# Linear attention feeding an MLP on one core: batch 0's k and v in nine-token rows, tails on alternate partitions, half of q moved to the weights' queue, and one weight block moved up in it

## The chip, the core and the metric

The kernel runs on one core of one Trainium2 chip. The metric is device time in microseconds (us) of that core for one call. A time is about 1.75 us longer than the span that the profile of the same execution shows (300.79 us and a span of 299.0 for the kernel before), so the two are never mixed here: "time" is the metric, "span" and every moment belong to a profile and count from the start of its span. Unless said otherwise, a moment is that of the one execution that was profiled.

## The reference, cut to what matters

```python
q, k, v: (8, 8, 576, 64) f32            # batch, heads, tokens, head size
phi(x) = concat(relu(x) * cos_w, relu(x) * sin_w)   # cos_w, sin_w depend on the token
q_p, k_p = phi(q), phi(k)
kv  = einsum('bhsf,bhsd->bhfd', k_p, v)
z   = sum over tokens of k_p
num = einsum('bhsf,bhfd->bhsd', q_p, kv)
den = einsum('bhsf,bhf->bhs', q_p, z) + 1e-6
x   = (num / den), heads side by side    # (4608, 512)
h   = x @ w_in                           # w_in (512, 2048)
out = relu(h)**2 @ w_out                 # w_out (2048, 512), out f32
```

576 tokens are four times 128 and 64 more. Those last 64 are the "tail" of each head.

## The kernel before

All products are in bf16. A fixed order of slots runs over eight batches: each slot is a piece of the first MLP product (`gemm1`, eight or ten slots for a batch) or of the second (`gemm2`), with pieces of the attention of later batches placed between them. Batch 0 has nothing to hide behind; its attention is the front of the kernel.

Loads come in three kinds. SyncE's queue brings k, v and q of batch 0. GpSimd's queue brings, in this order, the four blocks of w_in, then q, k, v of batch 1, then the four blocks of w_out, then batch 2. One small cast of v on GpSimd stands ahead of that queue as a gate, meant to hold its loads back behind those of batch 0: in the profile v landed at 11.24, the cast began at 11.29, and the queue's first load was issued at 11.73.

```python
    def load(src, nm, b, eng):
        main = inp.tile([P, H, J, D], F32, ...)      # token 4*p + j on partition p
        tail = inp.tile([P, HH, D], F32, ...)        # heads 0-3 on partitions 0-63, 4-7 on 64-127
        eng.dma_start(out=main, in_=src[b, :, 0:MAIN, :].rearrange("h (p j) d -> p h j d", j=J))
        for g in range(2):
            eng.dma_start(
                out=tail[g * TAIL : (g + 1) * TAIL, :, :],
                in_=src[b, g * HH : (g + 1) * HH, MAIN:S, :].rearrange("h p d -> p h d"),
            )
    ...
    with tc.manual_schedule():
        load_batch(0, nc.sync, "kvq")
        constants()
        warm(34)                                     # multiplies of zeros; the clock is 1.00 here
        for j in range(NS):
            att_k(0, j)
        att_v(0, J - 1, nc.gpsimd, H - 1, H)         # the gate
        ...
        for i in range(4):
            load_w1(i, 4)
        load_batch(1, nc.gpsimd, "qkv")
        for i in range(4):
            load_w2(i, 4)
        load_batch(2, nc.gpsimd, "qkv")
        att_kv(0, 0)
        att_kv(0, 1)
        ...                                          # q's features, num, x of the first half of batch 0
        for s in range(len(slots)):
            run(s)
```

The second product of batch 0 starts at slot 8. Slots 8 and 9 use w_out block 0 only; slot 10 is the first that uses block 1.

Of the kernel before, what the change touches and what calls it, by code (L numbers as in the profile page):

```python
# [15 lines left out]
FP = 512  # L16
# [3 lines left out]
def kernel(  # L20
# [37 lines left out]

    kqv = {}

    def load(src, nm, b, eng):
        main = inp.tile([P, H, J, D], F32, name=nm, tag=nm, bufs=2)
        tail = inp.tile([P, HH, D], F32, name=nm + "t", tag=nm + "t", bufs=2)
        eng.dma_start(  # L64
            out=main[:, :, :, :],
            in_=src[b, :, 0:MAIN, :].rearrange("h (p j) d -> p h j d", j=J),
        )
        for g in range(2):
            eng.dma_start(  # L69
                out=tail[g * TAIL : (g + 1) * TAIL, :, :],  # L70
                in_=src[b, g * HH : (g + 1) * HH, MAIN:S, :].rearrange("h p d -> p h d"),
            )
        kqv[nm, b] = (main, tail)

    def load_batch(b, eng, order):
        for nm in order:
            load({"k": k, "v": v, "q": q}[nm], nm, b, eng)

    def piece(nm, b, j):
        main, tail = kqv[nm, b]  # L80
        return main[:, :, j, :] if j < J else tail[:, :, :]
# [5 lines left out]
    cos_col = const.tile([P, J + 1], F32, name="cos_col")  # L87
    sin_col = const.tile([P, J + 1], F32, name="sin_col")

    def constants():  # L90
        sidx = const.tile([P, J + 1], F32, name="sidx")
        for p0, p1, c, n, base, mult in [
            (0, P, 0, J, 0, J),
            (0, TAIL, J, 1, MAIN, 1),
            (TAIL, P, J, 1, MAIN, 1),
        ]:
            nc.gpsimd.iota(
                sidx[p0:p1, c : c + n],
                pattern=[[1, n]],
                base=base,  # L100
                channel_multiplier=mult,
                allow_small_or_imprecise_dtypes=True,
            )
# [26 lines left out]
    vexts = []  # L130
    for i in range(2):
        vx = att.tile([P, J, H, E1], BF16, name=f"vext{i}")
        vxt = att.tile([P, HH, E1], BF16, name=f"vextt{i}")
        for t in (vx, vxt):
            ones = t[:, :, :, D:E1] if t is vx else t[:, :, D:E1]
            nc.vector.memset(ones, 1.0)
        vexts.append((vx, vxt))
    kps, kvzs, kzs, qps, tqs, qpTs, xs = {}, {}, {}, {}, {}, {}, {}
    nums, xts, xtails = {}, {}, {}
# [7 lines left out]
    def kp_of(b, j):  # L147
        if j == J:
            return cached(kps, (b, 1), [P, HH, F], "kpt", 1)
        return cached(kps, (b, 0), [P, J, H, F], "kp", 1)[:, j]  # L150
# [6 lines left out]
    def x_of(b, j):  # L157

        if j == J:
            return cached(xs, (b, 2), [P, 2, P], "xt", 2)  # L160
# [9 lines left out]
    def feat_cos(dst, src, j):  # L170
# [4 lines left out]
            scalar2=cos_col[:, j : j + 1],  # L175
# [4 lines left out]
    def feat_sin(dst, src, j):  # L180
        nc.scalar.activation(  # L181
            out=dst[:, :, D:F], in_=src, func=ACTF.Relu, scale=sin_col[:, j : j + 1]
        )
# [5 lines left out]
    def att_v(b, j, eng, h0=0, h1=H):  # L189
        copy = eng.copy if eng is nc.scalar else eng.tensor_copy  # L190
        vx, vxt = vexts[b % 2]
        if j == J:
            copy(out=vxt[:, :, 0:D], in_=piece("v", b, j))
        else:
            copy(out=vx[:, j, h0:h1, 0:D], in_=piece("v", b, j)[:, h0:h1, :])  # L195
# [9 lines left out]
    def fill(n):  # L205

        wm = ps_a.tile([P, 2, FP], F32, name="wm", tag="pa", bufs=1)
        for i in range(n):
            nc.tensor.matmul(
                out=wm[:, i % 2, :],  # L210
                lhsT=ident[:, :],
                rhs=zeros[:, :],
# [4 lines left out]
    def att_kv(b, part):  # L217
        vx, vxt = vexts[b % 2]
# [5 lines left out]



        for j in (0, 1) if part == 0 else range(2, NS):
            for hh in range(HH):
                for half in range(2):
                    h = half * HH + hh  # L230
                    if j < J:
                        lhsT, rhs = kp_of(b, j)[:, h, :], vx[:, j, h, :]
                    else:
                        p0, p1 = half * TAIL, (half + 1) * TAIL
                        lhsT, rhs = kp_of(b, j)[p0:p1, hh, :], vxt[p0:p1, hh, :]
                    nc.tensor.matmul(  # L236
                        out=kz[:, half, hh * E1 : (hh + 1) * E1],
                        lhsT=lhsT,
                        rhs=rhs,
                        start=(j == 0 and hh == 0),  # L240
                        stop=(j == J and hh == HH - 1),
                    )
        if part == 1:
            nc.scalar.copy(
                out=kvzs[b].rearrange("p (a h) e -> p a (h e)", a=2),
                in_=kz[:, :, 0 : HH * E1],
            )

    def att_feat(b, j, parts="cs"):
        for c in parts:  # L250
            f = feat_cos if c == "c" else feat_sin
            f(qp_of(b, j), piece("q", b, j), j)
# [15 lines left out]
    def att_qT_pe(b, j, apart=False):  # L268

# [3 lines left out]
        if apart:  # L273
            hi = ps_h.tile([P, HH, P], BF16, name="tqh", tag="hps", bufs=2)
            tqs[b, j].append(hi)
        elif nh == H:
# [14 lines left out]
    def att_num(b, j, early=False):  # L291
        qpT, kvz = qpTs[b, j], kvzs[b]
        if early:
            num = ps_h.tile([P, 2, FP], F32, name="num", tag="hps", bufs=2)
        else:
            num = ps_a.tile([P, 2, FP], F32, name="num", tag="pa", bufs=1)
# [321 lines left out]
```

## Time and profile before

| before | value |
|---|---|
| time, median of the first 3 executions | 300.75 us (300.23 to 300.79) |
| span of the profiled execution | 299.0 us |
| TensorE busy | 291.1 us, 97% of the span |
| VectorE, ScalarE, GpSimd busy | 46%, 51%, 16% |
| first `gemm1` multiply of batch 0 | 19.47 |
| first `gemm2` multiply, after a wait of 1.27 for w_out block 0 | 38.27 |
| slot 10, the first use of w_out block 1 | 41.74 |
| from there to the end of the span | 257.26 |

How to read it: TensorE is nearly always busy, so the time is the moment at which its unbroken train of multiplies starts plus the length of that train. The lines of the page that carry it stand in the prediction below.

### The profile page before, as it was taken

To read this page: it belongs to the slowest core of one execution; us is meant where nothing else is said; L and a number is where in the kernel's file an instruction comes from. 1 tells how busy PE (TensorE), PEld (TensorE's weight loads), DVE (VectorE), ACT (ScalarE), POOL (GpSimd) and SP (SyncE) were. 2 spreads that over 40 slices of the span, in tenths; PEclk is the share of its full clock that TensorE was granted. 3 is DMA by queue.
4 is the path that set the end of the run, shared out by engine and by line. 5 is a ranking of instruction groups with operands and counts; after the bars stand their busy time and mean duration, and the time that the engine had idled before them with its cause. 6 is when DMAs were issued, how large, how long until landed. Compare 5 with 4: busy or idle time off the path is not lost.

```text
span 299.0 us, 6477 instructions
## 1 busy us (share of the span) xinstructions
PE 291.1 (97%) x2701; PEld 202.3 (68%) x2701; DVE 136.6 (46%) x333; ACT 153.0 (51%) x213; POOL 47.8 (16%) x79
## 2 busy tenths in 40 slices
PE   8799989999999999999999999999999999999995
PEld 3379845889456984589654884589754894589544
DVE  2367654475648386228730287227740273024100
ACT  3465743666738554655554555555563552255311
POOL 1463404661121002000021001100021000100000
DMA  7999993999639987898568926898468115100021
GB/s 211 284 204 342 288 231 123 329 355 248 163 97 181 229 253 112 257 248 239 140 175 208 327 43 90 268 256 242 124 168 212 37 35 81 70 35 3 34 73 70
DMA packets 77069, 52.98 MB, mean 177 GB/s; under 512 B 52240, under 2 KB 71952, under 8 KB 77040
## 3 DMA queue, kind: packets, MB, share of 16 engines
q1 hardware_dynamic: 67120, 29.50, 42.2%
q0 software_dynamic: 9776, 22.94, 27.1%
q8 instruction: 21, 0.34, 0.5%
q10 hardware_dynamic: 144, 0.13, 0.1%
q14 instruction: 8, 0.07, 0.1%
HBM read 36.70 MB, written 9.44 MB: 154 GB/s over the span
## 4 chain that ended last, share of the span: by engine, by line
PE 86%; DMA 10%; POOL 1%; SPq 1%; issue 0%; ACT 0%; ACTq 0%
PE yps L413 40%; PE hps L378 38%; DMA q<-in_q_dram 5%; PE num L305 3%; DMA w2sb<-in_moe_w_out_dram 3%; DMA v<-in_v_dram 3%; PE kz L236 3%; PE yh L413 2%; POOL w1sb L117 1%; SPq L69 0%; PE tx L346 0%; PE tq L279 0%; POOL vt L69 0%; POOL vext L195 0%; SPq L64 0%
## 5 line engine op out<-in xcount | busy, mean ns | idle before, releaser
L378 PEld LDWEIGHTS <-w1sb 128*128 128x128 bf16 x1312 | 113.2, 98 | 12.1
L378 PE MATMUL hps<-xT,w1sb 128*128 128x256 bf16 (+1 forms) x1056 | 118.0, 269 | 0.0
L413 PE MATMUL yps<-w2sb,gT 128*128 128x512 bf16 (+1 forms) x496 | 110.4, 372 | 0.0
L386 ACT ACTIVATE rt<-hps 128x1024 bf16<-128x1024 f32 x72 | 73.7, 1024 | 59.2 <-DVE gT L393 32.8
L413 PEld LDWEIGHTS <-gT 128*128 128x128 bf16 x528 | 49.6, 98 | 54.0 <-DMA w2sb<-in_moe_w_out_dram 1.4
L393 DVE TENSOR_TENSOR gT<-rt 128x1024 bf16<-128x1024 bf16 x64 | 44.0, 688 | 82.8 <-ACT rt L386 82.8
L409 POOL DMA_DIRECT2D out_dram<-ysb x34 | 20.5, 605 | 176.2 <-ACT ysb L399 173.2
L399 ACT COPY ysb<-yps 128x512 f32<-128x512 f32 (+1 forms) x35 | 20.0, 575 | 55.3 <-PE yps L413 55.3
L181 ACT ACTIVATE qp<-q,sin_col 128x512 bf16<-128x512 f32 x32 | 21.9, 719 | 6.4 <-DMA q<-in_q_dram 6.4
L181 ACT ACTIVATE kp<-k,sin_col 128x512 bf16<-128x512 f32 x32 | 21.2, 714 | 3.1 <-DMA k<-in_k_dram 3.1
L319 DVE TENSOR_TENSOR x<-num,rden 128x512 bf16<-128x512 f32 x32 | 22.1, 691 | 1.1
L171 DVE TENSOR_SCALAR qp<-q,cos_col 128x512 bf16<-128x512 f32 x32 | 14.5, 492 | 11.7 <-DMA q<-in_q_dram 11.7
L315 DVE TENSOR_SCALAR den<-num 128x8 f32<-128x8 f32 (+1 forms) x40 | 6.6, 165 | 23.9 <-PE num L305 23.7
L171 DVE TENSOR_SCALAR kp<-k,cos_col 128x512 bf16<-128x512 f32 x32 | 15.1, 481 | 4.9 <-DMA k<-in_k_dram 4.9
L378 PE MATMUL hps<-xTt,w1sb 128*128 128x128 bf16 x256 | 15.3, 219 | 0.0
L413 PE MATMUL yps<-w2sb,gTt 128*128 128x512 bf16 x64 | 14.5, 379 | 0.0
L195 DVE CAST vext<-v 128x512 bf16<-128x512 f32 (+1 forms) x31 | 13.0, 425 | 2.9 <-DMA v<-in_v_dram 2.9
L305 PEld LDWEIGHTS <-qpT 128*128 128x128 bf16 (+1 forms) x240 | 10.3, 100 | 3.3 <-issue 1.7
L236 PEld LDWEIGHTS <-kp 128*128 128x128 bf16 x256 | 9.5, 97 | 4.4 <-issue 1.9
L201 PE MATMUL wm<-zeros 128*128 128x512 bf16 x42 | 10.9, 421 | 1.2 <-DVE zeros L86 1.2
L305 PE MATMUL num<-kvz,qpT 128*128 128x65 bf16 (+1 forms) x240 | 11.7, 194 | 0.0
L236 PE MATMUL kz<-vext,kp 128*128 128x65 bf16 x256 | 9.9, 193 | 1.6 <-DVE vext L195 1.6
(58 smaller groups left out, 132.6 us busy)
## 6 DMA issues: line engine op xcount, KB each, us to landing
out_dram<-ysb POOLq DMA_DIRECT2D x28, 256.0 KB, 3.9
k<-in_k_dram SPq DMA_DIRECT2D x5, 1024.0 KB, 6.2
v<-in_v_dram SPq DMA_DIRECT2D x5, 1024.0 KB, 6.7
q<-in_q_dram SPq DMA_DIRECT2D x5, 1024.0 KB, 5.9
q<-in_q_dram POOLq DMA_DIRECT2D x3, 1024.0 KB, 13.7
k<-in_k_dram POOLq DMA_DIRECT2D x3, 1024.0 KB, 10.1
v<-in_v_dram POOLq DMA_DIRECT2D x3, 1024.0 KB, 9.7
w1sb<-in_moe_w_in_dram POOLq DMA_DIRECT2D x4, 512.0 KB, 8.8
```

Of the source, the lines that this page charges most:

```text
L171: nc.vector.tensor_scalar(out=dst[:, :, 0:D], in0=src, scalar1=0.0, scalar2=cos_col[:, j : j + 1], op0=ALU.max, op1=ALU.mult,)
L181: nc.scalar.activation(out=dst[:, :, D:F], in_=src, func=ACTF.Relu, scale=sin_col[:, j : j + 1])
L195: copy(out=vx[:, j, h0:h1, 0:D], in_=piece("v", b, j)[:, h0:h1, :])
L236: nc.tensor.matmul(out=kz[:, half, hh * E1 : (hh + 1) * E1], lhsT=lhsT, rhs=rhs, start=(j == 0 and hh == 0), stop=(j == J and hh == HH - 1),)
L305: nc.tensor.matmul(out=out, lhsT=lhsT, rhs=kvz[:, half * HH + hh, :], start=True, stop=True)
L319: nc.vector.tensor_tensor(out=x_of(b, j).rearrange("p (b k) (l d) -> p b k l d", b=n, l=2), in0=n4[:, :, :, 0:D].rearrange("p b (k l) d -> ...
L378: nc.tensor.matmul(out=out, lhsT=w1sb[:, kb, hb * P : (hb + 1) * P], rhs=rhs, start=(kb == 0), stop=(kb == KB - 1),)
L386: nc.scalar.activation(out=rt[:, :, :], in_=hps[:, :, :], func=ACTF.Relu)
L393: nc.vector.tensor_tensor(out=dst, in0=rt[:, :, :], in1=rt[:, :, :], op=ALU.mult)
L399: nc.scalar.copy(out=ysb[:, c0:c1], in_=acc)
L409: eng.dma_start(out=dst, in_=ysb[p0 : p0 + n, c0:c1])
L413: nc.tensor.matmul(out=acc, lhsT=lhsT, rhs=w2sb[:, hb, c0:c1], start=(hb == 0), stop=(hb == HB - 1))
```

## The change

The intent is a faster front. k and v of batch 0 are loaded in rows of nine consecutive tokens (2304 bytes), 64 rows for each head, with heads 0 to 3 on even partitions and heads 4 to 7 on odd ones, so there are no separate tails and each load goes to every second partition. Because two heads then share one multiply, v is kept in two copies, each zero on the other head's partitions. q of batch 0 is split: the first half comes in four-token rows on SyncE's queue, the other half (0.52 MB) and q's tail (0.13 MB) move to GpSimd's queue. All tails of all batches go on alternate partitions too. Finally w_out block 0 moves ahead of k and v of batch 1. Cut to its core:

```diff
+    def load_tail(nm, b, eng):
         for g in range(2):
             eng.dma_start(
-                out=tail[g * TAIL : (g + 1) * TAIL, :, :],
+                out=tail_of(nm, b).rearrange("(p g) h d -> p g h d", g=2)[:, g],
                 in_=srcs[nm][b, g * HH : (g + 1) * HH, MAIN:S, :].rearrange("h p d -> p h d"),
             )
+    def load_rows(dst, src, n, h0, h1, eng):
+        for g in range(2):
+            eng.dma_start(
+                out=dst.rearrange("(p g) h j d -> p g h j d", g=2)[:, g, h0:h1],
+                in_=src[g * HH + h0 : g * HH + h1].rearrange("h (p j) d -> p h j d", j=n),
+            )
 ...
+    def of_half(eng, dst, src, g):                  # half_of is 1 on the partitions of half g, else 0
+        if eng is nc.scalar:
+            eng.activation(out=dst, in_=src, func=ACTF.Copy, scale=half_of[:, g : g + 1])
+        else:
+            eng.tensor_scalar_mul(out=dst, in0=src, scalar1=half_of[:, g : g + 1])
+    def v9(eng, h, g, j0=0, j1=J9):
+        of_half(eng, vext9(h)[:, g, j0:j1, 0:D], nine_of("v")[:, h, j0:j1, :], g)
 ...
-        load_batch(0, nc.sync, "kvq")
+        for nm, h0, h1 in (("k", 0, 2), ("k", 2, 4), ("v", 0, 2), ("v", 2, 3), ("v", 3, 4)):
+            load_nine(nm, h0, h1, nc.sync)
+        load_qa(nc.sync)
         constants()
+        ones_by_half()
-        warm(34)
+        warm(26)
 ...                                                 # features and masked copies by head pair
-        att_v(0, J - 1, nc.gpsimd, H - 1, H)
+        v9(nc.gpsimd, 2, 1, J9 - 1, J9)             # the gate, now on the third head pair of v
-        for i in range(4):
+        load_w1(0, 4)
+        load_qb(nc.gpsimd)
+        for i in range(1, 4):
             load_w1(i, 4)
-        load_batch(1, nc.gpsimd, "qkv")
-        for i in range(4):
+        load_batch(1, nc.gpsimd, "q")
+        load_w2(0, 4)
+        load_batch(1, nc.gpsimd, "kv")
+        load_tail("q", 0, nc.gpsimd)
+        for i in range(1, 4):
             load_w2(i, 4)
         load_batch(2, nc.gpsimd, "qkv")
 ...                                                 # kv of batch 0 in 36 multiplies of 130 columns,
                                                     # then q in four quarters of 64 tokens by 8 heads
```

## The prediction

> **What bounds the kernel now.** I read the windows view first, to see where TensorE is ever idle (columns: stretch, its length, then the busy time of each engine with its instruction count, clock, DMA share, GB/s).
>
> ```profile
> 0.00:1.20 1.20, 0.01 (x1) 0.01 (x1) 0.27 (x1) 0.00 (x0) 0.51 (x7) 1.00 0.00 0
> 1.20:11.75 10.55, 8.95 (x35) 3.67 (x36) 2.63 (x12) 5.13 (x9) 0.99 (x5) 1.00 0.95 294
> 11.75:19.47 7.72, 7.09 (x96) 4.40 (x95) 5.33 (x14) 4.95 (x9) 7.07 (x10) 1.00 1.09 197
> 19.47:37.00 17.53, 17.53 (x227) 16.03 (x224) 11.37 (x26) 10.95 (x14) 6.68 (x9) 1.00 1.13 299
> 37.00:38.27 1.27, 0.01 (x1) 0.00 (x0) 1.23 (x3) 1.27 (x3) 0.00 (x0) 1.00 1.25 208
> 38.27:60.00 21.73, 21.73 (x200) 13.62 (x201) 9.89 (x30) 9.96 (x17) 8.83 (x13) 1.00 0.84 229
> 60.00:126.50 66.50, 66.50 (x657) 45.77 (x655) 39.47 (x100) 40.59 (x60) 11.72 (x18) 1.00 0.87 210
> 126.50:278.40 151.90, 151.90 (x1401) 109.61 (x1400) 65.63 (x150) 76.04 (x97) 12.05 (x21) 1.00 0.59 149
> ```
>
> From 38.27 us to the last multiply TensorE has no gap at all, and the clock is full. So the kernel is a front of 38.27 us plus a fixed train of matmuls. A change to batch 0 is worth exactly the time by which that train starts earlier, and no more. Before 38.27 the multiplies that count are eight slots of the first MLP product of batch 0, from 19.47; warm-up and filler multiplies make up much of what precedes.
>
> Then the chain of waits (start, length, what), its early part:
>
> ```profile
> 2.70 8.54 DMA v<-in_v_dram
> 11.24 0.06 issue
> 11.29 0.50 POOL vext L195
> 11.79 3.08 POOL w1sb L117 x4
> 14.87 13.74 DMA q<-in_q_dram
> 28.61 0.28 issue
> 28.89 0.61 POOL vt L69
> 29.50 8.73 DMA w2sb<-in_moe_w_out_dram
> 38.23 0.05 issue
> 38.27 0.60 PE yh L413 x2
> ```
>
> The reader should see that attention of batch 0 is not on this chain. The chain is: v lands at 11.24; that releases one GpSimd cast, which gates the GpSimd DMA queue; this queue then moves w_in, batch 1 and w_out. TensorE's own order says the same (the bracket is idle time and its cause):
>
> ```profile
> 36.40 0.61 PE L279 MATMUL tq<-ident,qp 128*128 128x128 bf16 x8
> 38.27 0.60 PE L413 MATMUL yh<-w2sb,gT 128*128 128x512 bf16 x2 [1.27 <-DMA w2sb<-in_moe_w_out_dram]
> ```
>
> Making batch 0's attention faster alone would only lengthen this 1.27 us wait. What decides is when the weight blocks land.
>
> **Landing times before.** From issue times and times to landing (where two issues share one window, the answer gives their median, and I solve for the second): w_in blocks at 17.8, 20.5, 23.1, 25.6; q of batch 1 at 28.6 (tails 29.2); k at 32.4 (tails 32.85); v at 35.5 (tails 35.9); w_out blocks at 38.2, 40.8, 43.3, 45.9. So one weight block takes 2.5 to 2.6 us, a 1 MB batch tensor 2.65 to 3.2, a pair of tails 0.4 to 0.6. They land back to back: the queue is bandwidth-bound from about 14 us, when its first data flow, to 45.9.
>
> [...] 5.64 MB read between 25.6 and 40.8 is 371 GB/s, near the 351 GB/s of the SyncE loads at 7 to 12 us. [...] 351 GB/s at 3 to 5 us without tails, 278 at 5 to 7 us with 560 packets under 512 B. [...] The trace's x<-num multiply (N = 512) took 691 ns[...].
>
> **The change, part by part.**
>
> 1. SyncE loads. k and v come as nine-token rows of 2304 B: no separate tails, 2.36 MB; only half of q (0.52 MB) stays in this queue. Before, 3.54 MB ran from about 1.9 to 13.4 us, with 0.39 MB of tails costing 0.7 us more than large packets (0.39/0.22 - 0.39/0.37, an estimate from the rates above). Without that, 3.54 MB would take 10.8 us, 328 GB/s. With about 0.9 us from last byte to landing, estimates: first half of k 5.1, second 6.8, first half of v 8.4, the third head pair of v (which gates GpSimd) 9.1, last 10.1, half of q 11.7. Before: k 6.4, v 11.26, q 14.36.
>
> 2. Feature work. VectorE now does six two-input passes over 576 elements[...], and four masked copies at about 0.45 (a 512-element cast took 0.42): 6.3 us, begun at 5.1 with short waits, done near 11.7. ScalarE's nine small activations and four masked copies fit beside it. kv is 36 multiplies of 130 columns instead of 40 of 65, some 2 us, mostly hidden. Then the q part in four quarters: before, q landing to first MLP multiply took 19.47 - 14.36 = 5.1 us; quarters pipeline it but have more links, so I keep 5.1 from 11.8. First MLP multiply at 16.9, a gain of 2.6 us.
>
> 3. GpSimd queue. v gates it at 9.1, cast about 0.45, so w_in block 0 is issued at 9.55 instead of 11.73 and lands 6.1 later, 15.65. Behind it now comes the other half of q (0.52 MB in 512 B runs, about 1.75 us, estimated from half of a batch tensor and some loss). So the other w_in blocks land at 20.0, 22.55, 25.05: only 0.5 us earlier than before. Slots 1 to 3 of the first product want them at about 19.9, 22, 24.8. Hence slot 3 starts at about 25.1 (26.35 before): the gain shrinks from 2.6 to about 1.3 here.
>
> 4. w_out block 0 moves ahead of k and v of batch 1: it lands at 25.05 + 3.0 + 0.6 + 2.4 = 31. Slot 3 to the end of the first product took 36.99 - 26.35 = 10.64, so w_out is wanted at 35.7; the 1.27 us wait goes. But block 1 still stands behind k, v, their tails and now also q's tails of batch 0: 31 + 3.2 + 0.45 + 2.7 + 0.4 + 0.5 + 2.5 = 40.8. It is wanted two slots of 1.73 us after 35.7, at 39.2. Before, that slot began at 38.27 + 3.46 = 41.73 with its block there at 40.8. So the wait moves from block 0 to block 1: 1.6 us of new wait, and the train is 41.73 - 40.8 = 0.9 us ahead of before.
>
> 5. After that, block 2 lands near 43.3 and is wanted after 45; no wait. Tails of the other seven batches: 4 multiplies of 130 columns for 8 of 65, even; two ScalarE copies of kv for one, a masked VectorE copy more: beside TensorE. Batch 2's q load now waits until q's tail of batch 0 is used (about 48 us, was issued at 34.1), lands near 54 and is wanted near 59. No cost, but the margin shrinks.
>
> [...]
>
> **Rivals.**
> (a) The front gain passes through whole: 2.6 + 1.27 = 3.9 us, 296.9 us. For it: w_out block 0 really is early. Against: w_in and w_out block 1 land hardly earlier, as the back-to-back landings say.
> (b) w_out block 1 does not bind, only w_in: slot 10 at 39.2, gain 2.5, 298.2 us. It needs the queue 1.6 us faster than I add it up[...].
> (c) v lands no earlier than before[...], so block 1 lands at 42 or later: gain 0 or a loss of up to 1 us.
> (d) VectorE's 6.3 us, or a semaphore chain among the quarters, delays the first multiply beyond 19.5. It would take an error over 2.6 us; unlikely, and up to 1 us of it is free because w_in binds.
> (e) The program orders each GpSimd transfer behind the landing of the one eight before it (before, kt waited 2.0 us for w_in this way). w_out block 1 now waits so for k of batch 1; if nothing else is queued meanwhile, the queue runs dry for up to 1 us. v and the tails should cover it.
>
> **Range and chances.** 300.75 - 1.1 gives 299.6. Full success of (b) gives the low end, 298.2; (c) and (e) in part give the high end, 300.8. Two per cent is 6 us, more than the whole front gain of (a), and a loss of 6 us would need a new stall in the steady part: faster 0.01, same 0.98, slower 0.01.
>
> **What would show it right or wrong.** Right: v's third part releases GpSimd near 9.1 to 9.6; the first MLP multiply near 17; a TensorE wait on w_in of some tenths before slots 1 to 3; no wait before the first yh multiply, near 35.7; a wait of 1 to 2 us on w_out before the second block, near 40.8; and no gap afterwards. Wrong: a first MLP multiply later than 18.5; no w_out wait at all (then (b) or (a)); a wait on k or v of batch 1 or on q of batch 2; TensorE gaps after 60 us; or strided tail weights that lengthen the tail groups of eight multiplies beyond their 0.25 us.

The marks in it stand for passages that are cut because no trace or run of this case shows what they say. Step 2's 6.3 us was six passes at 0.757 us and four copies at 0.45; the changed kernel's six passes took 0.748 to 0.759 each in its trace. Step 4's sum comes to a gain of 0.9 us (299.85); terms that are cut rounded it up to 1.1 us, and so to the 299.6 of the range. The rate behind 0.39/0.22 in step 1 stands nowhere above it; the nearest measured one is 211 GB/s, from 5.8 to 6.0 us, where 110 of the 126 packets were under 512 B. The "about 0.9 us from last byte to landing" fits q, whose queue moved data until about 13.4 and which landed at 14.36. The "some 2 us" for kv fits the 1.73 us that eight multiplies of 512 columns take in this trace: at that rate 36 of 130 columns would take 1.98.

## The result, and the profile after

The changed kernel is correct. Its time is 301.58 us, median of 4 executions (300.69 to 301.85), against 300.50 (300.23 to 300.79) for the kernel before in the same rounds. The ratio is 1.0031, with a 95% interval of 1.0006 to 1.0055. A ratio here is always the mean time of one kernel's fast executions over that of the other's of the same rounds, so it is not quite the ratio of the medians quoted. The class is "same", as predicted; the size is not: a gain of 1.1 us was predicted, and a small loss came, outside the range.

The profiled execution was the changed kernel's fastest one (300.69; span 298.9). The windows view of the changed kernel, in the stretches shown of the kernel before (columns: stretch, length, busy time and instruction count of TensorE, its weight loads, VectorE, ScalarE and GpSimd, then clock, DMA share, GB/s), with two finer stretches at the end:

```profile
1.20:11.75 10.55, 8.10 (x36) 3.60 (x37) 6.86 (x22) 7.11 (x16) 2.37 (x8) 0.98 0.84 273
11.75:19.47 7.72, 7.18 (x95) 5.89 (x94) 4.97 (x13) 3.21 (x8) 6.68 (x9) 0.80 1.04 200
19.47:37.00 17.53, 17.06 (x219) 15.59 (x218) 12.40 (x32) 11.66 (x16) 6.27 (x10) 1.00 1.13 290
37.00:38.27 1.27, 1.27 (x16) 1.09 (x15) 0.83 (x3) 0.71 (x2) 0.60 (x1) 1.00 1.06 233
...
8.60:11.06 2.46, 0.01 (x2) 0.00 (x1) 2.46 (x5) 1.98 (x3) 1.02 (x2) 1.00 0.93 306
11.06:15.70 4.64, 4.64 (x46) 4.37 (x46) 2.63 (x5) 2.72 (x7) 4.64 (x7) 0.63 0.88 157
```

Two things are new. The hole at 37.00 to 38.27 is filled, as predicted. And the clock, which was 1.00 throughout before, is 0.80 in the second stretch. The finer rows show where: from 8.60 to 11.06 TensorE did nothing, while VectorE was busy all the time; in the 4.6 us after it, TensorE ran at a mean clock of 0.63 (it was 0.50 from 11.37 to 14.79). That the idle time brought this about is tested by warm38 below. TensorE's timeline of the changed kernel (start, length, group, and in the bracket the idle time before it and what ended it):

```profile
11.06 1.87 PE L338 MATMUL kz<-vext,kp 128*128 128x130 bf16 x18 [2.45 <-DVE vext L232]
...
20.20 0.61 PE L600 MATMUL hps<-xT,w1sb 128*128 128x128 bf16 x8 [0.46 <-ACT xT L465]
...
37.99 0.38 PE L639 MATMUL yh<-w2sb,gT 128*128 128x512 bf16 x1
...
41.85 0.59 PE L639 MATMUL yh<-w2sb,gT 128*128 128x512 bf16 x2
```

and slot 10 on TensorE's timeline of the kernel before:

```profile
41.74 0.59 PE L413 MATMUL yh<-w2sb,gT 128*128 128x512 bf16 x2
```

The first `gemm1` multiply comes at 20.20, 0.7 us later than before and 3.3 us later than predicted. The second product starts at 37.99 with no wait. Slot 10 starts at 41.85 without a wait, 0.11 us later than before. So the train has gained nothing.

The early chain of waits of the changed kernel, taken from a query that ends at 21 us (start, length, what), shows what leads to that late first multiply:

```profile
2.87 4.50 DMA k<-in_k_dram
...
7.47 1.58 DVE kp L304 x3
9.04 0.44 issue
9.48 1.54 DVE vext L232 x2
11.02 0.04 issue
11.06 1.87 PE kz L338 x18
...
14.74 0.62 PE kzh L338 x9
...
18.45 0.59 ACT qpTp L430
```

The second half of k lands at 7.37 (VectorE had waited 1.17 us for it), VectorE works through features and masked copies until 11.02, kv runs at the low clock until 15.36, and only then do the steps of q follow. q's first half had landed by 12.4 (two transfers, at 11.7 and 12.4): it is not on this chain. VectorE's timeline shows the size of the masked copies in the changed kernel:

```profile
9.48 1.52 DVE L232 TENSOR_SCALAR vext<-v,half_of 128x576 bf16<-128x576 f32 x2
```

and of the plain casts in the kernel before:

```profile
11.26 1.14 DVE L195 CAST vext<-v 128x512 bf16<-128x512 f32 x3 [2.92 <-DMA v<-in_v_dram]
```

Two copies of 576 elements take 1.52, so 0.76 each; three casts (two of 512 elements and one of 448, which the group's line hides) take 1.14, so 0.38 each, as they overlap a little (one lasts 0.41 to 0.47 by itself). GpSimd's timeline in the changed kernel gives the queue:

```profile
9.95 0.45 POOL L232 TENSOR_SCALAR vext<-v,half_of 128x64 bf16<-128x64 f32 x1 [8.02 <-DMA v<-in_v_dram]
...
35.35 2.24 POOL L198 DMA_DIRECT2D w2sb<-in_moe_w_out_dram  x3 [2.44 <-DMA k<-in_k_dram]
48.91 0.90 POOL L99 DMA_DIRECT2D q<-in_q_dram  x1 [11.31 <-DVE qp L277]
```

The gate opens at 9.95 rather than 9.1. w_in block 0, issued at 10.48, lands at 16.2; the moved half of q at 17.9; the last w_in block at about 26.1; q of batch 1 at 29.2; w_out block 0 at 32.0; k of batch 1 at 35.1. w_out block 1, issued at 35.35, takes 6.5 to land: about 41.8. That is the very moment at which slot 10 starts. Two ends therefore meet there: TensorE reaches slot 10 at about 41.8, and the block lands at about 41.8.

### The profile page after: what moved, and what is told of

Its sections match the earlier page's. It is cut to its first block, busy times and chain, and to the rows that moved or that the text cites. A ratio compares the mean times of both kernels' runs of the same rounds, so it can differ in the third digit from the quotient of the medians.

```text
span 298.9 us, 6467 instructions
## 1 busy us (share of the span) xinstructions
PE 289.2 (97%) x2655; PEld 204.2 (68%) x2677; DVE 144.6 (48%) x357; ACT 154.6 (52%) x229; POOL 50.3 (17%) x87
## 3 DMA queue, kind: packets, MB, share of 16 engines
q0 software_dynamic: 10016, 23.60, 29.2%
## 4 chain that ended last, share of the span: by engine, by line
PE 93%; DVE 2%; DMA 2%; ACT 1%; issue 1%; SPq 1%; ACTq 0%; DVEq 0%
PE hps L600 42%; PE yps L639 39%; PE num L514 3%; PE kz L385 2%; PE yh L639 2%; DMA k<-in_k_dram 2%; PE tq L491 1%; SPq L108 1%; PE kz L338 1%; PE kz L396 1%; PE kzh L338 1%; DVE kp L304 1%; PE tx L566 1%; DVE vext L232 1%; PE kz L365 0%
## 5 line engine op out<-in xcount | busy, mean ns | idle before, releaser
L639 PE MATMUL yps<-w2sb,gT 128*128 128x512 bf16 (+1 forms) x476 | 107.7, 372 | 1.2 <-DVE qpTp L500 0.2
L287 ACT ACTIVATE qp<-q,sin_col 128x512 bf16<-128x512 f32 (+1 forms) x34 | 22.3, 693 | 7.5 <-DMA q<-in_q_dram 7.5
L287 ACT ACTIVATE kp<-k,sin_col 128x512 bf16<-128x512 f32 (+1 forms) x35 | 21.5, 670 | 0.0
L277 DVE TENSOR_SCALAR qp<-q,cos_col 128x512 bf16<-128x512 f32 (+1 forms) x34 | 15.3, 485 | 11.5 <-DMA q<-in_q_dram 11.5
L277 DVE TENSOR_SCALAR kp<-k,cos_col 128x512 bf16<-128x512 f32 (+1 forms) x35 | 15.9, 453 | 0.0
L300 DVE CAST vext<-v 128x512 bf16<-128x512 f32 x28 | 11.8, 421 | 0.0
L514 PE MATMUL num<-kvz,qpT 128*128 128x65 bf16 (+1 forms) x240 | 11.7, 194 | 0.0
L639 PEld LDWEIGHTS <-gTt 128*128 128x128 bf16 x64 | 6.3, 98 | 7.5
L385 PEld LDWEIGHTS <-kp 128*128 128x128 bf16 x224 | 8.5, 97 | 2.4
L639 PE MATMUL yh<-w2sb,gT 128*128 128x512 bf16 x30 | 9.1, 379 | 0.1
```

The source lines that it names most:

```text
L277: nc.vector.tensor_scalar(out=dst[:, :, 0:D], in0=src, scalar1=0.0, scalar2=cos_col[:, c : c + 1], op0=ALU.max, op1=ALU.mult,)
L287: nc.scalar.activation(out=dst[:, :, D:F], in_=src, func=ACTF.Relu, scale=sin_col[:, c : c + 1])
L300: nc.vector.tensor_copy(out=vext_of(b, j)[:, :, 0:D], in_=piece("v", b, j))
L385: nc.tensor.matmul(out=kz[:, a, c0 : c0 + E1], lhsT=kp_of(b, j)[:, h, :], rhs=vext_of(b, j)[:, h, :], start=(j == 0 and c == 0 and g == 0) ...
L514: nc.tensor.matmul(out=out, lhsT=lhsT, rhs=kvz[:, half * HH + hh, :], start=True, stop=True)
L639: nc.tensor.matmul(out=acc, lhsT=lhsT, rhs=w2sb[:, hb, c0:c1], start=(hb == 0), stop=(hb == HB - 1))
```

## The experiments

The theory after reading the result: the mechanism of the prediction is right (the time is the start of slot 10 plus a fixed train), but two chains both end too late, the front because of the masked copies and the lost clock, and w_out block 1 because the queue ahead of it is longer than added up. Then repairing one of them should gain nothing. Rivals: the loss is VectorE's masked copies alone; the lost clock alone; the late gate alone; the reorder of w_out; or something in the steady part. Twelve runs were made in four calls; the kernel before was run beside them in each call (medians 300.61, 300.49, 301.08, 300.57). All twelve were correct.

This table collects the moment that the argument turns on. Span minus slot 10 is the length of the rest of the train; each row is one profiled execution.

| kernel | first `gemm1` multiply | wait for w_out block 1 | slot 10 starts | span | span minus slot 10 |
|---|---|---|---|---|---|
| before | 19.47 | none (1.27 for block 0) | 41.74 | 299.0 | 257.3 |
| changed | 20.20 | none | 41.85 | 298.9 | 257.1 |
| after_again | 20.75 | none | 42.38 | 299.4 | 257.0 |
| split8 | 20.28 | 0.85 | 42.92 | 300.0 | 257.1 |
| warm38 | 19.10 | 1.60 | 42.65 | 300.6 | 258.0 |
| w2b | 19.13 | none | 40.76 | 298.6 | 257.8 |
| before_w2up | 18.70 | none | 39.90 | 297.2 | 257.3 |
| gate_v0 | 18.92 | 1.10 | 42.80 | 300.4 | 257.6 |
| combo | 18.29 | 1.63 | 42.12 | 299.1 | 257.0 |
| qb_twice | 20.67 | 1.25 | 44.51 | 301.6 | 257.1 |
| q_sync | 20.14 | 0.99 | 42.92 | 299.6 | 256.7 |
| q_sync_warm | 19.14 | none | 40.80 | 297.5 | 256.7 |
| no_reorder | 21.98 | 1.83 for block 0 | 45.27 | 302.3 | 257.0 |
| w2up_spare | 18.40 | 0.37 | 41.59 | 298.9 | 257.3 |

Slot 10 ranges over 5.4 us, from 39.90 to 45.27, while the rest stays between 256.7 and 258.0. In the profiled executions, that rules out a cost of the change in the steady part: the two profiles of the changed kernel have 257.1 and 257.0, less than the 257.3 before. (warm38, w2b and gate_v0 have 0.5 to 0.9 us more in the rest, each in its one profiled execution.)

### after_again: the changed kernel, unchanged

No edit; it shows how much the changed kernel scatters.

> The changed kernel, unchanged, to see how it varies: its first profile was its fastest execution (300.69 us; the other three 301.45 to 301.85). There the second w_out block landed at 41.85 us, just when TensorE came to it. Theory B (two ends meet: the train of matmuls waits either for the first MLP product or for w_out block 1, whichever is later): a slower execution shows a TensorE wait of 0.5 to 1 us on w2sb near 42 us. Theory A (only the slow start of the first product counts): a slower execution shows the first hps multiply later than 20.2 us, and no w2sb wait. Median 301 to 301.8, ratio 1.001 to 1.004.

Measured: 301.21 us (301.01 to 302.15, 6 executions), ratio 1.0027 (1.0005 to 1.0048). The profiled execution has its first multiply at 20.75 and slot 10 at 42.38, with no wait for w_out, whose block 1 landed at about 42.2. Here the front is what ends last, by 0.2 us; in the first profile the two met. The small loss is real (the interval leaves out 1), and its two ends lie within half a microsecond of each other.

### split8: VectorE's masked copies cut into eight rows and one

```diff
     def v9(eng, h, g, j0=0, j1=J9):
-        of_half(eng, vext9(h)[:, g, j0:j1, 0:D], nine_of("v")[:, h, j0:j1, :], g)
+        cuts = [(j0, j1)] if eng is not nc.vector else [(0, J9 - 1), (J9 - 1, J9)]
+        for a, z in cuts:
+            of_half(eng, vext9(h)[:, g, a:z, 0:D], nine_of("v")[:, h, a:z, :], g)
```

> VectorE's four masked nine-row copies are cut into 8 rows and 1 row. They took 0.76 us each where 8-row casts take 0.42. Expected: 8-row part about 0.42 to 0.45, 1-row part 0.12 to 0.2, so kv starts at 10.3 to 10.7 instead of 11.06, and the first hps multiply comes 0.4 to 1.5 us before 20.2 (the larger figure if TensorE keeps its full clock). Theory A: the time falls by the same. Theory B: w_out block 1 still lands near 41.9, so the time stays within 0.3 us of the changed kernel, and a w2sb wait of the size of the head start appears near 42 us.

Measured: 302.09 us (301.69 to 302.61), ratio 1.0052 (1.0029 to 1.0076). From VectorE's timeline of this kernel:

```profile
10.35 1.20 DVE L232 TENSOR_SCALAR vext<-v,half_of 128x512 bf16<-128x512 f32 x4
```

and from TensorE's:

```profile
42.92 0.59 PE L641 MATMUL yh<-w2sb,gT 128*128 128x512 bf16 x2 [0.85 <-DMA w2sb<-in_moe_w_out_dram]
```

Four shorter copies take 1.20 where two long ones took 1.52, and the stretch from VectorE's first pass over the second half of k to the first kv multiply is 3.11 instead of 3.59. So the nine-row copies do cost what the trace says, yet the time did not fall: slot 10 was ready at 42.07 by TensorE's order and waited 0.85 for the block. The rival "masked copies alone" falls, since the block came last here. The expectation of an earlier front missed, though: in this execution k's second half landed at 8.2 instead of 7.4, so kv began at 11.44 and the first multiply came at 20.28, no earlier than in the changed kernel. What the copies are worth in the front was therefore not seen at the first multiply. The time is also some 0.9 us above the changed kernel's, where at most 0.3 was expected. In this kernel the gate's cast took 0.85 instead of 0.45 on GpSimd, so the queue was released later.

### warm38: 38 warm-up multiplies instead of 26

```diff
-        warm(26)
+        warm(38)
```

> 38 warm-up multiplies instead of 26, so TensorE is not idle from 8.6 to 11.06 us. Expected: granted clock 1.0 in 11 to 15 us (it was 0.5 from 12 to 14), kv and its fillers take about 3 us instead of 4.5, and the first hps multiply comes at 18.5 to 19.2 instead of 20.2. If the clock drop was only a side effect of VectorE being late anyway, less than 0.4 us moves. Theory A: the time falls by 1 to 1.7 us. Theory B: it falls by less than 0.3 us, with a w2sb wait near 42 us.

Measured: 301.69 us (301.44 to 302.33, 5 executions), ratio 1.0038 (1.0016 to 1.0061). From the windows of this kernel, its kv stretch:

```profile
11.59:14.60 3.01, 3.01 (x44) 2.86 (x44) 2.49 (x5) 2.33 (x6) 3.01 (x5) 1.00 0.77 93
```

and TensorE's timeline:

```profile
19.10 0.61 PE L600 MATMUL hps<-xT,w1sb 128*128 128x128 bf16 x8 [0.46 <-ACT xT L465]
...
42.65 0.59 PE L639 MATMUL yh<-w2sb,gT 128*128 128x512 bf16 x2 [1.60 <-DMA w2sb<-in_moe_w_out_dram]
```

The clock is 1.00, kv with its fillers takes 3.0 us instead of 4.6, and the first multiply comes 1.1 to 1.65 us earlier than in the two profiles of the changed kernel. The gain went into the 1.60 us wait for w_out block 1. The rival "lost clock alone" falls as well; so says the changed kernel's one execution that kept a mean clock of 1.0, too: it took 301.45, in the middle of the 300.69 to 302.15 of its nine others. (This execution of warm38, its slowest, also lost some 0.9 us after slot 10; where was not found.)

### w2b: w_out block 1 moved ahead of v of batch 1

```diff
-        load_batch(1, nc.gpsimd, "kv")
+        load_batch(1, nc.gpsimd, "k")
+        load_w2(1, 4)
+        load_batch(1, nc.gpsimd, "v")
         load_tail("q", 0, nc.gpsimd)
-        for i in range(1, 4):
+        for i in range(2, 4):
             load_w2(i, 4)
```

and, so that v is not wanted too early, kv of batch 1 goes from slot 10 to 11, its first two `num` steps from 11 and 13 to 12 and 13, and the first transpose of x from 12 to 13.

> w_out block 1 moved ahead of v of batch 1 in the GpSimd queue; kv of batch 1 one slot later, and its first num and transpose one slot later, to allow for v's later landing. The front is untouched, so the first hps multiply stays at 20.2. w_out block 1 lands about 3 us earlier, near 38.5, and v near 42. Theory B: the slow executions vanish, median about 300.7 (0.8 below the changed kernel), no w2sb wait. Theory A: unchanged, 301.4 to 301.7. If v is now late, a wait on vext appears before kz near 45 us.

Measured: 300.89 us (300.37 to 301.97), ratio 1.0015 (0.9989 to 1.0040). Block 1 landed at 38.2 and nothing waits for it. The six executions fall in two groups: 300.37, 300.42 and 300.42 at clocks of 0.997 to 1.000, and 301.35, 301.87 and 301.97 at 0.994. So the slow executions did not vanish, as had been expected. A drop to 0.50 for 3.4 us takes about 0.6% off the mean over 300 us, which is the 0.994. With the block out of the way the time is set by the front, and the front depends on the clock. Its profiled execution is a fast one: there TensorE's warm-ups lasted longer (until 9.89 instead of 8.61), it idled 1.69 us before kv instead of 2.45, and the clock held. The other profiles agree. After an idle time before kv of 1.69 us or less (warm38 0.55, gate_v0 1.19, the kernel before 1.60) the clock stayed at 1.00 there; after 2.18 (q_sync), 2.25 (split8), 2.45 and 3.03 (the changed kernel), 2.47 (qb_twice) and 3.83 (no_reorder) it fell to 0.50 for 3.4 us or more. So in these kernels the lost clock goes with how long the idle time before kv happens to be. The rest of the train was some 0.7 us longer here, with a wait of 0.67 in a `num` step of batch 1 that the moved slots brought.

### before_w2up: the kernel before, with only w_out block 0 moved up

```diff
-        load_batch(1, nc.gpsimd, "qkv")
-        for i in range(4):
+        load_batch(1, nc.gpsimd, "q")
+        load_w2(0, 4)
+        load_batch(1, nc.gpsimd, "kv")
+        for i in range(1, 4):
             load_w2(i, 4)
```

> The kernel before with the reorder alone: w_out block 0 ahead of k and v of batch 1. Block 0 then lands near 31 and the 1.27 us wait of TensorE on w2sb before the first yh goes, so the first yh comes at 37.0. Block 1 still lands near 40.8 (the same bytes in front of it as before); it is wanted at 37.0 + 3.46 = 40.46. Theory B (landing of w_out block 1 sets the train): a w2sb wait of about 0.4 us before the second block, time 0.9 us below before, 299.7. Theory A (the wait of 1.27 was the only cost): 299.3, no w2sb wait. A rival: the wait moves whole, time as before.

Measured: **299.35 us** (298.99 to 299.92), ratio 0.9944 (0.9903 to 0.9986). This beats both kernels: 1.14 us under the 300.49. TensorE's timeline of this kernel:

```profile
18.70 1.95 PE L378 MATMUL hps<-xT,w1sb 128*128 128x128 bf16 x32
...
39.90 0.59 PE L413 MATMUL yh<-w2sb,gT 128*128 128x512 bf16 x2
...
41.63 1.14 PE L236 MATMUL kz<-vext,kp 128*128 128x65 bf16 x32
```

kv of batch 1, which follows slot 10 and needs v of batch 1, starts at 41.63 with no bracket, so nothing waited: not for w_out block 1 (issued at 29.51, landed at 39.6, wanted at 39.90) and not for the delayed v. The one wait of TensorE between 17 and 50 us is 0.2 us on a VectorE copy. The reorder did what step 4 of the prediction says for block 0, and here block 1 is just in time. In this profile, its fastest execution, the first multiply also came 0.77 us earlier than in the profile of the kernel before, which the edit does not touch; so the 1.14 us of the medians, and not the 1.84 us between the two slots 10, is the measure of what the reorder is worth.

### gate_v0: GpSimd's gate on the first half of v

```diff
-        for g in range(2):
-            v9(act, 1, g)
+        v9(act, 1, 0)
+        v9(act, 1, 1, 0, J9 - 1)
 ...
-        v9(nc.gpsimd, 2, 1, J9 - 1, J9)
+        v9(nc.gpsimd, 1, 1, J9 - 1, J9)
```

(and the two masked copies of the third head pair on ScalarE whole).

> In the changed kernel the GpSimd cast that gates the weight queue reads the first half of v (heads pairs 0 and 1) instead of the third head pair; the copy of the third goes to ScalarE. In the traces so far the DMA engines are almost idle for 1.5 to 2 us between the last SyncE load (11.5) and the first weights (13.1 to 13.6). Expected: w_in block 0 issued at 9.3 to 9.8 instead of 10.5 to 11.2, all later landings 0.8 to 1.1 us earlier, w_out block 1 at 41 to 41.8. The first hps multiply stays at 19 to 20.7, depending on the clock. Theory B: no w2sb wait left, time 0.3 to 0.9 us below the changed kernel. Theory A: time unchanged.

Measured: 301.28 us (301.01 to 303.07), ratio 1.0016 (0.9967 to 1.0065). The expectation missed. The gate did open earlier, at 9.06, but its cast took 0.84 (0.45 in the changed kernel), and w_in block 0, issued at 9.85, landed only at about 17.3, later than the 16.2 of the changed kernel. TensorE waited 0.36 and 0.20 for w_in and 1.10 for w_out block 1. Around that issue the DMA engines moved 244 GB/s from 10 to 11 us and 214 from 11 to 12, against 320 and 165 in the changed kernel; which queue's data these were, the windows do not say. So opening the gate earlier is no repair, but the run can't clear the late gate either, since w_in did not come earlier; why it came 1.1 us later was not settled.

### combo: gate_v0, warm38 and split8 together, and q's tail of batch 0 behind w_out block 1

The edits of the three, and in the queue:

```diff
         load_batch(1, nc.gpsimd, "kv")
+        load_w2(1, 4)
         load_tail("q", 0, nc.gpsimd)
-        for i in range(1, 4):
+        for i in range(2, 4):
             load_w2(i, 4)
```

> All of it in the changed kernel: earlier gate, 38 warm-up multiplies, 8+1 row masked copies, and the tail of batch 0's q moved behind w_out block 1. If both ends are what counts (theory B), both move: first hps multiply near 18.7 to 19, w_out block 1 at 40.3 to 41, slot 10 at about 40.6 against 41.73 in the kernel before: 299.3 to 299.8, about 0.8 us below before and 1.7 below the changed kernel. Theory A alone would give a gain of 1.5 over the changed kernel too, but with no part played by the queue; the runs before this one tell those apart. If some third thing sets the end, the time stays above 300.6.

Measured: 301.09 us (300.84 to 301.28), ratio 0.9999 (0.9958 to 1.0041); in medians 0.6 above the kernel before. A miss. TensorE's timeline:

```profile
42.12 0.59 PE L641 MATMUL yh<-w2sb,gT 128*128 128x512 bf16 x2 [1.63 <-DMA w2sb<-in_moe_w_out_dram]
```

The first multiply is at 18.29, the earliest of any kernel here, and the wait for block 1 takes 1.63 back. The gate's cast lasted 1.16. Repairing the front, however far, does not help while the queue is this long.

### qb_twice: the moved half of q loaded twice

```diff
         load_qb(nc.gpsimd)
+        scratch = const.tile([P, H, 2 * D], F32, name="scratch")
+        nc.gpsimd.dma_start(
+            out=scratch.rearrange("p h (j d) -> p h j d", j=2),
+            in_=q[0, :, QA:MAIN, :].rearrange("h (p j) d -> p h j d", j=2),
+        )
```

> The load of batch 0's second half of q (0.52 MB in 512 B runs, GpSimd queue, between w_in blocks 0 and 1) is issued twice, the second into a scratch tile that nothing reads. What it costs the queue is the shift of the later landings: I had estimated 1.75 us; the landings of the changed kernel (w_in block 0 to block 3 in 10.2 us, three blocks at 2.57 in the kernel before make 7.7) give 2.5 us. Expected: w_in blocks 1 to 3 and w_out block 0 land 2.3 to 2.6 us later than in the changed kernel (1.75 if my first estimate holds), TensorE waits on w1sb, and the time is 2 to 3 us longer.

Measured: 303.37 us in its one execution (state unknown), beside 300.49. This measures the disputed cost. Against after_again the last w_in block lands at 28.7 instead of 26.5, w_out block 0 at 34.6 instead of 32.3, k of batch 1 at 37.7 instead of 35.4. So 0.52 MB in runs of 512 bytes costs what follows in this queue 2.2 to 2.3 us, some 235 GB/s, where the prediction had 1.75. (In the changed kernel q of batch 1, 1.05 MB in 1 KB runs, landed 3.1 us behind the block before it: 29.2 less 26.1, some 340 GB/s.) TensorE's timeline shows it arrive undiminished at slot 10:

```profile
44.51 0.59 PE L639 MATMUL yh<-w2sb,gT 128*128 128x512 bf16 x2 [1.25 <-DMA w2sb<-in_moe_w_out_dram]
```

44.51 is 2.1 us behind after_again, and its span is 2.2 longer.

### q_sync: the half of q and its tail back on SyncE's queue

```diff
         load_qa(nc.sync)
+        load_qb(nc.sync)
+        load_tail("q", 0, nc.sync)
 ...
         load_w1(0, 4)
-        load_qb(nc.gpsimd)
 ...
-        load_tail("q", 0, nc.gpsimd)
```

> The changed kernel with the second half of batch 0's q and its tail put back into the SyncE queue, behind the first half, as all of q was before; nothing else moved. Theory Q (what spoiled the gain is 0.65 MB of q put into the GpSimd queue ahead of w_out block 1): w_in block 3 lands near 24.2 (26.4 to 26.8 in the changed kernel), w_out block 1 near 39.5 (41.85 to 42.9), no w2sb wait. The time is then set by the first hps multiply, 19 to 20.7 by the clock that TensorE happens to have: 299.5 to 301, median about 300.3. Rival: [...]w_in block 0 lands later by the same amount and w_out block 1 stays near 42: 301.2.

Measured: 300.81 us (300.28 to 301.43), ratio 0.9993 (0.9978 to 1.0009), so 0.27 under the kernel before in medians, where the changed kernel was 0.6 and 1.1 above. Moving 0.65 MB out of GpSimd's queue thus gave about 0.9 to 1.4 us, less than theory Q expected (a median of 300.3) and more than its rival (301.2). The profiled execution, the slowest one, shows the rival's way: w_in block 0 now landed at about 18.9, while the DMA engines moved 306 and 287 GB/s from 12 to 14 us (39 and 164 in the changed kernel), and w_out block 1, issued earlier at 31.02, took 11.9 to land:

```profile
42.92 0.59 PE L639 MATMUL yh<-w2sb,gT 128*128 128x512 bf16 x2 [0.99 <-DMA w2sb<-in_moe_w_out_dram]
```

Up to the last w_in block, which landed at 26.5 as in after_again, the bytes counted in that execution, not the queue that carried them. That does not explain block 1, though: it landed 3.7 us behind the last tail in front of it (39.2), where the changed kernel took 2.2 (39.6 to 41.8).

### q_sync_warm: the same with 38 warm-up multiplies

The edits of q_sync and of warm38.

> The same with 38 warm-up multiplies, so that TensorE keeps its clock (in the changed kernel this alone moved the first hps multiply from 20.2 to 19.1 and was eaten by a 1.6 us wait on w_out block 1). Theory Q: now both ends move: first hps multiply 19.1 or less, slot 10 near 40.6, no w2sb wait, 299.3 to 299.7, some 1.7 us below the changed kernel and about equal to the kernel before with the reorder alone (299.35). Rival: a w2sb wait near 42 remains and the time stays at 301.2 to 301.7.

Measured: 300.65 us, but from 299.30 to 301.81, all at a clock of 1.0; ratio 0.9991 (0.9968 to 1.0014). The profiled execution is the fastest: first multiply at 19.14, block 1 landed at 40.8, slot 10 at 40.80 without a wait:

```profile
40.80 0.59 PE L639 MATMUL yh<-w2sb,gT 128*128 128x512 bf16 x2
```

That is the moment that the prediction gave for slot 10, and its 299.30 is close to the predicted 299.6. In the new layout only one other profile reached slot 10 that early: w2b's (40.76), in which block 1 had been moved up and the clock happened to hold. Both ends were right in both. Even so, only two of the six executions here met the expected 299.3 to 299.7. What makes the others up to 2.5 us slower, with the same clock, is not explained: only one execution was profiled.

### no_reorder: the change with w_out block 0 back behind k and v of batch 1

```diff
         load_batch(1, nc.gpsimd, "q")
-        load_w2(0, 4)
         load_batch(1, nc.gpsimd, "kv")
         load_tail("q", 0, nc.gpsimd)
-        for i in range(1, 4):
+        for i in range(4):
             load_w2(i, 4)
```

> The changed kernel with w_out block 0 put back behind k and v of batch 1: all of the change but the reorder. The same bytes then stand before w_out block 0 as before block 1 now, less one block: it lands near 39.5, wanted at 37 to 38.5; block 1 near 42, wanted two slots later, 43. So a w2sb wait of 1 to 2.5 us before the first yh, slot 10 at 43 against 41.73 in the kernel before: 301.8 to 302.3, 1.3 to 1.8 us above before. With the reorder alone at -1.15 this would make the parts nearly add up to the whole (+0.7). If instead it stays at 300.5 to 301.2, the reorder does nothing in this kernel.

Measured: 303.57 us (302.82 to 304.55), ratio 1.0086 (1.0067 to 1.0105).

```profile
41.80 0.39 PE L639 MATMUL yh<-w2sb,gT 128*128 128x512 bf16 x1 [1.83 <-DMA w2sb<-in_moe_w_out_dram]
```

On TensorE's timeline the second product waits 1.83 for block 0 and begins 3.5 us later than in the kernel before. So the change without the reorder loses 2.5 us in medians to the kernel before; the changed kernel with it lost 0.6 and 1.1, so the reorder is worth 1.4 to 1.9 us within the change. The front of this execution was the worst of all: TensorE idled 3.83 us before kv, the mean clock was 0.987, and the first multiply came at 21.98. Part of the loss in this one trace is therefore the front's, and the time is above the 301.8 to 302.3 expected.

### w2up_spare: the better kernel, with the moved part of q loaded besides

Does the extra load in GpSimd's queue alone undo the reorder's gain? This is before_w2up with 0.52 MB of q (same tokens, same 512-byte runs) loaded into a spare tile after w_in block 0, and q's tail (0.13 MB) ahead of w_out block 1; nobody reads them.

```diff
+        spare = const.tile([P, H, 2, D], F32, name="spare")
+        spare_t = const.tile([P, HH, D], F32, name="spare_t")
+        load_w1(0, 4)
+        nc.gpsimd.dma_start(out=spare[:, :, :, :],
+            in_=q[0, :, 256:MAIN, :].rearrange("h (p j) d -> p h j d", j=2))
-        for i in range(4):
+        for i in range(1, 4):
             load_w1(i, 4)
 ...
         load_batch(1, nc.gpsimd, "kv")
+        for g in range(2):
+            nc.gpsimd.dma_start(out=spare_t[g * TAIL : (g + 1) * TAIL, :, :], in_=...)
         for i in range(1, 4):
```

> The kernel before with the reorder (299.35, first hps multiply 18.7, w_out block 1 landed at 39.6 with no wait), plus one suspected cost alone: the 0.65 MB of batch 0's q which the change put into the GpSimd queue, loaded there at the same places (0.52 MB in 512 B runs behind w_in block 0, two tail pieces ahead of w_out block 1) into spare tiles that nothing reads. The front stays as it was before. If those bytes are what took the reorder's gain away: w_in block 3 near 27.3, w_out block 1 near 42.3 (39.6 + 2.2 as the doubled load cost + 0.5), a w2sb wait of 1.5 to 2.5 us or waits on w1sb, time 1.8 to 2.7 above the reorder alone, 301.1 to 302. If the queue has slack, or the loss comes from the changed front, the time stays at 299.3 to 300.

Measured: 301.76 us (300.68 to 302.50), ratio 1.0051 (1.0034 to 1.0067). Against the kernel before it is 1.19 above, where before_w2up was 1.14 below: 2.3 us for 0.65 MB. TensorE's timeline, in its fastest execution:

```profile
21.63 1.92 PE L378 MATMUL hps<-xT,w1sb 128*128 128x256 bf16 x16 [0.39 <-DMA w1sb<-in_moe_w_in_dram]
...
41.59 0.59 PE L413 MATMUL yh<-w2sb,gT 128*128 128x512 bf16 x2 [0.37 <-DMA w2sb<-in_moe_w_out_dram]
```

With a front of the old kind and its first multiply at 18.40, the waits are now on w_in (three, 0.9 us together) and on w_out block 1. None of the new layout is in it, and the extra bytes alone bring it to where the changed kernel is. One caveat: SyncE's full load of q is still in it, so it bears 0.65 MB more in all than the changed kernel does.

## Why the prediction was wrong

**The frame held.** "The time is a front plus a fixed train" is what the table shows. The wait did leave w_out block 0 and w_out block 1 did become the next bound. Rival (a), the whole gain passing through, and rival (e), the queue running dry, did not come: block 1 was issued at 35.35, while transfers ahead of it were landing until 39.6. Step 5 held too: q of batch 2 was issued at 48.91 (about 48 said), landed at 56.6 rather than 54, and nothing waited for it; the rest of the train is even 0.2 us shorter with the new tails (257.1 against 257.3, and so in after_again and qb_twice; the cause was not examined).

**Step 1 failed, and with it the gate of step 3.** It took "0.39 MB of tails costing 0.7 us more than large packets" out of SyncE's queue. By 8 us that queue had moved 1.7 MB in both kernels. The new loads begin at about 2.3 us instead of 1.9 and dip to between 134 and 249 GB/s at 4 to 5.5 us, so long rows on alternate partitions saved nothing by then. The step's reading of the trace was thin: it held the tails to cost more because the stretch at 5 to 7 us ran at 278 GB/s with 560 small packets, but the stretch at 7 to 12 us, which it quotes at 351, had 562 of them too. k's second half landed at 7.4 and 8.1 in the two profiles instead of 6.8, and VectorE waited 1.17 and 1.75 us for it. The gate opened at 9.95 and 10.50 instead of 9.1, and w_in block 0 landed at 16.2 and 16.7 instead of 15.65. This is the outcome of rival (c), "block 1 lands at 42 or later: gain 0 or a loss of up to 1 us", but not its reason: v did land earlier than before, only by some 0.8 to 1.3 us at the gate instead of 2.2. No run changes these loads, so whether their rows, their partitions or the number of issues is to blame stays open.

**Step 3's half of q was mis-sized.** 1.75 us was said; qb_twice measured 2.2 to 2.3. (This half did land about 1.75 us behind w_in block 0; the rest shows in the blocks behind it.) From w_in block 0 to the last one it took 9.9 and 9.8 us instead of 9.4. Together with the late gate, the last w_in block landed at 26.1 and 26.5 rather than 25.05, and everything behind it shifted: w_out block 1 at 41.8 and 42.2 rather than 40.8. The sum in between, step 4's, was right: 15.7 us in both profiles against 15.75. So of the 1.0 and 1.4 us by which block 1 was late, the gate brought 0.5 and 1.1, and the w_in stretch with q in it the rest. That alone turns the predicted lead of 0.9 into a lag of 0.1 to 0.4. What the step overlooked is its sign as a whole: the queue that sets the next bound was given 0.65 MB more to carry. w2up_spare prices that load by itself at 2.3 us, more than the whole gain hoped for.

**Tails.** On alternate partitions the tails came no sooner behind their tensor: k's landed 0.5 after k (35.1 to 35.6), 0.45 before.

**Step 2 failed in three terms.** First, the "four masked copies at about 0.45" took 0.76 each, 1.2 us more in all. The number came from a cast of 512 elements; the copy is of nine rows of 64. What makes it longer was not shown. By shape, in these traces: the masked copy of 576 elements lasts 0.80 by itself (two take 1.52, as they overlap), a two-input pass over the same 576 elements 0.755, a masked copy of 256 elements 0.35, and split8's copy in two pieces, of eight rows and of one, 0.60 in its first group (two in 1.20) and 0.69 in its second (two in 1.38). I had read the duration of another shape. Second, the step saw kv "mostly hidden" and never asked whether TensorE's clock would survive a front in which it has nothing to do; 2.45 us of idle time and 1.6 us of slow kv followed (4.6 against 3.0). Third, "q landing to first MLP multiply" was kept at 5.1 us from 11.8, but q landed at 12.4 and the chain begins where kv ends, at 15.4, and 4.8 us follow. Hence 20.20 and 20.75 instead of 16.9. Rival (d), a first multiply beyond 19.5, was called "unlikely"; it came true in both profiles, and with it the sign of being wrong, "a first MLP multiply later than 18.5".

**Why neither failure shows alone.** The front made slot 10 ready at 41.8 to 42.4, and the queue delivered its block at 41.8 to 42.2. Repairing the front (warm38, combo) moved its gain into the wait; repairing the queue (w2b) left the front and its clock in charge. Where both were right in the same execution (q_sync_warm's fastest, and w2b's profile), slot 10 was at 40.80 and 40.76, the moment predicted. The other executions of q_sync_warm, at the same clock, were slower by up to 2.5 us, so the two repairs are not shown to be enough.

**What stays open.** Executions of one kernel scatter by about 1 us, once by 2.5, without a difference in clock; the traces at hand show the second half of k landing anywhere from 7.4 to 8.6 and block 1 from 40.8 to 42.9, but not why. Why an earlier gate brought w_in block 0 later, and what shortened the rest of the train by 0.2 us, is open too.

## What to carry to other kernels

When a kernel's start is bound by a queue of loads, work out what a change adds to that queue ahead of the next bound before counting what it takes off the compute side: here a reorder alone gained 1.14 us, and 0.65 MB put into the same queue cost 2.3. Follow every chain that ends near the same moment, since repairing one of two only lengthens the wait for the other. Take an operation's duration from its own shape, and look at what a shorter, idler front does to TensorE's clock: in the profiles here it fell to 0.50 after 2.18 us or more of idle time before kv, and stayed at 1.00 after 1.69 or less.
